# Issuing the TensorE and VectorE work of a full-attention loop in written order, score matmuls and PV matmuls each in one group per key tile

## The chip, the cores and the metric

The kernel runs on one core of a Trainium2 chip. The metric is the device time of one execution in microseconds (us), and a quoted time is the median of several executions. The mean granted TensorE clock, a fraction of full speed, is listed with each execution. Runs of one batch share a chip and the runs of the kernel before. TensorE is "PE" in the profile, VectorE is "DVE", ScalarE is "ACT", GpSimd is "POOL".

## The reference, cut to what matters

The program is four layers with residuals: a local dilated attention (A), a full attention with one shared key and value head (B), and the same two again. Only B is touched by the change. It has 2048 tokens, 32 query heads of 16 dimensions and one key/value head:

```python
def _B_ref(x, wq, wk, wv, wo):
    ...
    q = (x @ wq).reshape(B, S, H, Dh).transpose(0, 2, 1, 3)     # S = 2048, H = 32, Dh = 16
    k = x @ wk                                                  # one key head for all
    v = x @ wv
    scores = jnp.einsum("bhqd,bkd->bhqk", q, k) * (Dh ** -0.5)
    p = _softmax(scores, axis=-1)
    o = jnp.einsum("bhqk,bkd->bhqd", p, v)
    return o.transpose(0, 2, 1, 3).reshape(B, S, H * Dh) @ wo

x = x + _A_ref(_layernorm(x), A_wqkv, A_wo)
x = x + _B_ref(_layernorm(x), B_wq, B_wk, B_wv, B_wo)
x = x + _A_ref(_layernorm(x), A_wqkv, A_wo)
x = x + _B_ref(_layernorm(x), B_wq, B_wk, B_wv, B_wo)
```

## The kernel before

Each B layer is a loop of 512 steps: 32 blocks (512 queries of four heads each) times 16 key tiles of 128 keys. Per step the engines do this:

- TensorE computes four score tiles, each in its own quarter of the array's rows. Three go into a PSUM tile `st`, one into `dv`.
- ScalarE takes the exponential of the three in one instruction: `pt = exp(st)`.
- VectorE takes the fourth head's exponential by integer arithmetic. A "fix" (`tt` from `dv`, 512 columns) is done every step. A "pass" (`it` from `tt`, 2048 columns, covering four steps' fixes) is also done every step, four passes with different offsets for each group of four key tiles.
- TensorE multiplies by the values (PV): three matmuls of `pt` and four of `it`, each in its own quarter of the array's columns, all accumulating into `o_ps`.

So a step has 4 score and 7 PV matmuls, one exponential, one fix and one pass. There are two `st` buffers, one `dv` buffer and one `o_ps` buffer.

At the end of each block `finish_block` copies `o_ps` out on VectorE and sends the denominators on by DMA. After each second block it takes their reciprocals on VectorE and sends them out by DMA again, for a multiplication on GpSimd. The end of some blocks is followed by four output-projection matmuls ("y") and the addition of their result on VectorE.

The instructions are written in a sensible order, but in the kernel before they only carry data dependencies: the scheduler of the kernel language decides at build time in what order each engine gets them.

```python
def order_after(tc, inst, pred):
    if inst is not None and pred is not None:
        same = inst.ins.engine == pred.ins.engine
        tc.add_manual_dep(inst.ins, pred.ins.name, _ORDER if same else _AFTER, reason="issue order")
```

```python
    def emit_scores(s):
        b, kt, gd = where(s)
        qc, t, a = blocks[b]
        st = st_tiles[s] = stp.tile([128, 3, 512], F32, name="st")
        dv = dv_tiles[s] = dvp.tile([128, 512], F32, name="dv")
        outs = [(g, st[:, n, :]) for n, g in enumerate(g for g in range(4) if g != gd)] + [(gd, dv[:])]
        for g, out in outs:
            nc.tensor.matmul(out, lhsT=KAB[32 * g:32 * g + 32, a, kt * 128:(kt + 1) * 128],
                             rhs=QT[32 * g:32 * g + 32, t, qc * 512:(qc + 1) * 512],
                             start=True, stop=True, tile_position=(32 * g, 0))

    def emit_exp(s):
        pt = pt_tiles[s] = ptp.tile([128, 3, 512], BF16, name="pt")
        nc.scalar.activation(out=pt[:], in_=st_tiles.pop(s)[:], func=AF.Exp, scale=scale)

    def emit_fix(s):
        m, r = divmod(s, 4)
        if r == 0:
            t_tiles[m] = ttp.tile([128, 4, 512], I16, name="tt")
        nc.vector.tensor_scalar(out=t_tiles[m][:, r, :], in0=dv_tiles.pop(s)[:], scalar1=T_SCALE, scalar2=T_BIAS,
                                op0=ALU.mult, op1=ALU.add)

    def emit_pass(m, j):
        it = i_tiles[(m, j)] = itp.tile([128, 4, 512], BF16, name="it")
        nc.vector.tensor_scalar(out=it[:].bitcast(I16), in0=t_tiles[m][:], scalar1=0.25,
                                scalar2=127.0 * 128.0 + J_OFF[j], op0=ALU.mult, op1=ALU.add)
        if j == NJ - 1:
            del t_tiles[m]

    def pv(b, g, kt, j, rhs, stop):
        if b not in o_ps:
            o_ps[b] = opp.tile([128, 512], F32, name="o_ps")
        nc.tensor.matmul(o_ps[b][32 * g:32 * g + 32, :], lhsT=VE[:, kt, j, :], rhs=rhs,
                         start=(b, g) not in started, stop=stop, tile_position=(0, 32 * g))
        started.add((b, g))

    def emit_pv_act(s):
        b, kt, gd = where(s)
        pt = pt_tiles.pop(s)
        for n, g in enumerate(g for g in range(4) if g != gd):
            pv(b, g, kt, 0, pt[:, n, :], False)

    def emit_pv_dve(m, j):
        b, kt0, _ = where(4 * m)
        it = i_tiles.pop((m, j))
        for r in range(4):
            pv(b, r, kt0 + r, j, it[:, r, :], kt0 + 4 == NT and j == NJ - 1)

    # ... finish_block (the copy, the DMAs, the reciprocal) and emit_y cut ...
```

```python
    # ... pump() cut: it takes up to `budget` entries of the queue that are ready ...
    emit_scores(0)
    emit_fix(0)
    emit_scores(1)
    for s in range(nsteps + 8):
        if s < nsteps:
            emit_exp(s)
        if s + 1 < nsteps:
            emit_fix(s + 1)
        if s + 2 < nsteps:
            emit_scores(s + 2)
        m, j = divmod(s - 3, 4)
        if 0 <= s - pv_lag < nsteps:
            queue.append(("act", s, s - pv_lag))
        if 0 <= m < nsteps // 4:
            queue.append(("dve", s, (m, j)))
            if j == NJ - 1 and m % 4 == 3:
                queue.append(("end", s + 1, m // 4))
        if queue and queue[0][0] == "end":
            pump(s, 1)
        if 0 <= m < nsteps // 4:
            emit_pass(m, j)
        pump(s, pv_budget)
    while queue:
        pump(10 ** 9, 100)
    for qi in range(4):
        emit_y(NQC - 1, qi, (opp, dvp)[qi % 2], ("o_ps", "dv")[qi % 2])
```

`order_after` exists already. Between two instructions of one engine it fixes their order and adds no semaphore.

Of the kernel before, what the change touches and what calls it, by code (L numbers as in the profile page):

```python
# [8 lines left out]
I16 = mybir.dt.int16  # L9
# [467 lines left out]
def attn_B_fast(ctx, tc, QT, KAB, VE, wo_sb, x_sb, S, tag, out_dram=None, on_qc_done=None, st_bufs=2,  # L477
                pv_lag=3, y_gap=2, pv_budget=4):
    nc = tc.nc
# [20 lines left out]
    st_tiles, dv_tiles, pt_tiles, t_tiles, i_tiles = {}, {}, {}, {}, {}  # L500
    o_ps, started = {}, set()
    x_pair, onc = {}, {}

    def emit_scores(s):
        b, kt, gd = where(s)
        qc, t, a = blocks[b]
        st = st_tiles[s] = stp.tile([128, 3, 512], F32, name="st")
        dv = dv_tiles[s] = dvp.tile([128, 512], F32, name="dv")
        outs = [(g, st[:, n, :]) for n, g in enumerate(g for g in range(4) if g != gd)] + [(gd, dv[:])]
        for g, out in outs:  # L510
            nc.tensor.matmul(out, lhsT=KAB[32 * g:32 * g + 32, a, kt * 128:(kt + 1) * 128],  # L511
                             rhs=QT[32 * g:32 * g + 32, t, qc * 512:(qc + 1) * 512],
                             start=True, stop=True, tile_position=(32 * g, 0))

    def emit_exp(s):
        pt = pt_tiles[s] = ptp.tile([128, 3, 512], BF16, name="pt")
# [2 lines left out]
    def emit_fix(s):  # L519
        m, r = divmod(s, 4)  # L520
        if r == 0:
            t_tiles[m] = ttp.tile([128, 4, 512], I16, name="tt")
        nc.vector.tensor_scalar(out=t_tiles[m][:, r, :], in0=dv_tiles.pop(s)[:], scalar1=T_SCALE, scalar2=T_BIAS,  # L523
                                op0=ALU.mult, op1=ALU.add)

    def emit_pass(m, j):
        it = i_tiles[(m, j)] = itp.tile([128, 4, 512], BF16, name="it")
        nc.vector.tensor_scalar(out=it[:].bitcast(I16), in0=t_tiles[m][:], scalar1=0.25,  # L528
                                scalar2=127.0 * 128.0 + J_OFF[j], op0=ALU.mult, op1=ALU.add)
        if j == NJ - 1:  # L530
            del t_tiles[m]

    def pv(b, g, kt, j, rhs, stop):
        if b not in o_ps:
            o_ps[b] = opp.tile([128, 512], F32, name="o_ps")
        nc.tensor.matmul(o_ps[b][32 * g:32 * g + 32, :], lhsT=VE[:, kt, j, :], rhs=rhs,  # L536
                         start=(b, g) not in started, stop=stop, tile_position=(0, 32 * g))
        started.add((b, g))

    def emit_pv_act(s):  # L540
# [11 lines left out]
    def finish_block(b):  # L552
        qc, t, a = blocks[b]
        ops = o_ps.pop(b)
        if a == 0:
            X = nrm.tile([128, 512], F32, name="X")
            S2 = nrm.tile([128, 2, 16], F32, name="S2")
            x_pair[b // 2] = (X, S2)
            nc.vector.tensor_copy(out=X[:], in_=ops[:])  # L559
            src = X  # L560
        else:
            X, S2 = x_pair.pop(b // 2)
            src = nrm.tile([128, 512], F32, name="X1")
            nc.vector.tensor_copy(out=src[:], in_=ops[:])
        for g in range(4):
            nc.sync.dma_start(out=S2[32 * g:32 * g + 32, a, :], in_=src[32 * g + 16:32 * g + 17, :])  # L566
        if a == 0:
            return
        for g in range(4):
            nc.sync.dma_start(out=X[32 * g + 16:32 * g + 32, :], in_=src[32 * g:32 * g + 16, :])  # L570
        nc.vector.reciprocal(out=S2[:], in_=S2[:])
        rd = drm.tile([4, 2, 512], F32, name="rd")
        for g in range(4):
            nc.sync.dma_start(out=rd[g].rearrange("a (c e) -> c a e", e=16), in_=S2[32 * g:32 * g + 32, :, :])
        lb = nrm.tile([128, 512], F32, name="lb")
        for g in range(4):
            for aa in range(2):
                nc.sync.dma_start(out=lb[32 * g + 16 * aa:32 * g + 16 * aa + 16, :],
                                  in_=rd[g, aa:aa + 1, :].to_broadcast([16, 512]))
        if t == 0:  # L580
            onc[qc] = nrm.tile([128, 4, 512], BF16, name="onc")
        nc.gpsimd.tensor_tensor(out=onc[qc][:, t, :], in0=X[:], in1=lb[:], op=ALU.mult)  # L582
# [3 lines left out]
    def emit_y(qc, qi, pool, name):  # L586
        y = pool.tile([128, D], F32, name=name)
        for t in range(4):
            nc.tensor.matmul(y[:], lhsT=onc[qc][:, t, qi * 128:(qi + 1) * 128], rhs=wo_sb[:, t, :],  # L589
                             start=(t == 0), stop=(t == 3))  # L590
        qt = 4 * qc + qi
        if out_dram is not None:
            if qi == 0:
                xo[qc] = nrm.tile([128, 4, D], BF16, name="xo")
            nc.vector.tensor_tensor(out=xo[qc][:, qi, :], in0=x_sb[:, qt, :], in1=y[:], op=ALU.add)  # L595
        else:
            nc.vector.tensor_tensor(out=x_sb[:, qt, :], in0=x_sb[:, qt, :], in1=y[:], op=ALU.add)
        if qi == 3:
            del onc[qc]
            if out_dram is not None:  # L600
# [2 lines left out]
            if on_qc_done is not None:  # L603
                on_qc_done(qc)

    queue = []
    held = [0]

    def pump(now, budget):
        n = 0  # L610
# [21 lines left out]
    emit_fix(0)  # L632
    emit_scores(1)
    for s in range(nsteps + 8):
        if s < nsteps:
            emit_exp(s)
        if s + 1 < nsteps:
# [11 lines left out]
            pump(s, 1)  # L649
        if 0 <= m < nsteps // 4:  # L650
            emit_pass(m, j)
        pump(s, pv_budget)
    while queue:
        pump(10 ** 9, 100)
    for qi in range(4):
        emit_y(NQC - 1, qi, (opp, dvp)[qi % 2], ("o_ps", "dv")[qi % 2])


@with_exitstack
# [181 lines left out]
```

## Time and profile before

| | kernel before |
|---|---|
| time, four runs | median 1969.22 us (1967.03 to 1971.10) |
| first B loop, from first to last exponential | 734.8 us in the profiled execution, 1.435 us a step |
| second B loop | 736.1 us |
| between the loops (output projection, layer A, set-up of B) | 232.1 us |
| after the second loop | 27.8 us |

The profiled execution took 1960.04 us.

From the page of the kernel before: the busy time of each engine, and the chain of work that ended last by engine.

```profile
PE 1737.2 (89%) x14596; PEld 520.2 (27%) x14596; DVE 1672.4 (85%) x2657; ACT 1569.1 (80%) x1261; POOL 76.0 (4%) x104
...
DVE 44%; PE 41%; issue 6%; ACT 4%; SPq 2%; DMA 2%; POOL 1%; DVEq 0%; POOLq 0%; ACTq 0%
```

From the view of windows, the part of the first loop in which the mean clock rounds to 1.00 (one dip to 0.50, of 3.4 us at 655 us, lies in it). The columns are the window, its length, then the busy time (and number of instructions) of PE, PEld, DVE, ACT and POOL, then the granted clock, the DMA share and GB/s.

```profile
250.00:960.00 710.00, 664.51 (x5506) 155.22 (x5505) 665.32 (x1076) 684.45 (x498) 19.61 (x15) 1.00 0.05 10
```

TensorE is busy 664.51 of 710 us (94%), VectorE 94%, ScalarE 96%. None is full, and all three are close. The chain of waits says who hands over to whom. It is from 400 to 900 us, by line of the kernel: L511 is the score matmul, L517 the exponential, L523 the fix, L528 the pass, L536 the PV matmul.

```profile
by line: DVE tt L523 25.1%; DVE it L528 23.3%; PE o_ps L536 18.6%; PE dv L511 11.5%; PE st L511 8.3%; ACT pt L517 3.9%; issue 3.2%; SPq L566 1.6%; DVE X L559 0.6%; DVE st_next L50 0.6%; DMA S_7801<-X_8106 0.6%; DVE x_sb L597 0.4%; DMA S_907
```

The exponential, on ScalarE, is 3.9% of this chain. The chain goes to and fro between VectorE (48%) and TensorE (38%). The waits of the same stretch are listed as us in total, number of times, and the longest:

```profile
DVE tt L523 <- PE dv L511: 25.2, 53, 0.8
ACT pt L517 <- PE st L511: 18.4, 30, 1.0
PE dv L511 <- DVE tt L523: 17.4, 38, 0.9
```

Here VectorE waits for TensorE's `dv` and TensorE waits for VectorE's fix, in many short waits. The timeline shows what the scheduler's order looks like. The columns are start, length, engine, line, operation and tiles, and the count; lines of weight loads are left out.

```profile
1239.85 0.38 PE L511 MATMUL dv<-QT,KAB 32*128 32x512 bf16 x1
...
1240.16 0.40 PE L536 MATMUL o_ps<-it,VE 128*32 128x512 bf16 x4
1240.27 0.69 DVE L523 TENSOR_SCALAR tt<-dv 128x512 int16<-128x512 f32 x1 [0.17 <-PE dv L511]
...
1240.50 0.39 PE L511 MATMUL st<-QT,KAB 32*128 32x512 bf16 x3
...
1240.82 0.39 PE L536 MATMUL o_ps<-pt,VE 128*32 128x512 bf16 x1
1240.88 1.28 DVE L528 TENSOR_SCALAR it<-tt 128x2048 int16<-128x2048 int16 x2
...
1241.14 0.39 PE L511 MATMUL dv<-QT,KAB 32*128 32x512 bf16 x1
...
1241.46 0.39 PE L536 MATMUL o_ps<-pt,VE 128*32 128x512 bf16 x2
1241.46 0.60 PE L536 MATMUL o_ps<-it,VE 128*32 128x512 bf16 x4
...
1242.00 0.39 PE L511 MATMUL st<-QT,KAB 32*128 32x512 bf16 x3
1242.08 0.68 DVE L523 TENSOR_SCALAR tt<-dv 128x512 int16<-128x512 f32 x1
```

A single `dv` matmul stands alone at 1239.85. Four PV matmuls follow, then three `st`, one PV, one more `dv` alone, six PV, and three `st`. Each of these groups takes about 0.32 us until the next one starts (0.54 for the six), although up to four members of a group run side by side in the array. TensorE never stands still here: from this `dv` to the one two steps later, at 1242.86, it takes 3.01 us, 1.5 a step. On VectorE two passes follow each other (1240.88, x2) instead of a fix and a pass in turn, so the fix of the `dv` made at 1241.14 comes only at 1242.08, when the passes are done.

Last, ScalarE's own pace. The prediction takes it from a stretch of the timeline without a listed wait:

```profile
494.08 20.31 ACT L517 ACTIVATE pt<-st 128x1536 bf16<-128x1536 f32 x15 [0.49 <-PE st L511]
```

Fifteen exponentials took 20.31 us, and the last of them counts with its full recorded 1.45, so they start (20.31 - 1.45) / 14 = 1.347 us apart on average. This mean is not the floor. Of the 14 distances eleven are 1.330 to 1.335, two are 1.35, and one is 1.485 (from 506.08 to 507.56). That last one waited for its `st` matmuls, which ran from 507.06 to 507.45, but no wait is listed, because the record of the exponential before it is 1.54 us long and covers the gap. In the changed kernel, the first exponentials of these two lines are 16 steps apart:

```profile
247.94 2.87 ACT L522 ACTIVATE pt<-st 128x1536 bf16<-128x1536 f32 x2
269.22 3.08 ACT L522 ACTIVATE pt<-st 128x1536 bf16<-128x1536 f32 x2
```

That is 21.28 / 16 = 1.330 us from start to start. In both kernels this is by far the most frequent distance (within 5 ns, 393 of 1023 before and 828 after), and none is below 1.329. So 1.330 us is the floor of a step as long as ScalarE does this work.

### The profile page before, as it was taken

How to read it: one execution, taken by the hardware profiler on the slowest of the kernel's cores; microseconds unless marked ns; L12 is line 12 of the kernel's file. 1: busy time of each engine (PE TensorE's matmuls, PEld its weight loads, DVE VectorE, ACT ScalarE, POOL GpSimd, SP SyncE). 2: the span in 40 equal slices, each digit the busy share in tenths (PEclk: the TensorE clock that was granted, in tenths of full speed). 3: DMA queues.
4: the chain of work that ended last, by engine and by line, in shares of the span. 5: the costliest groups of instructions: out<-in, count | busy, mean ns of one | idle time of the engine just before them, and what ended most of it. 6: DMA issues, size and time to landing. Idle time of an engine off the chain costs nothing.

```text
span 1958.3 us, 35782 instructions
## 1 busy us (share of the span) xinstructions
PE 1737.2 (89%) x14596; PEld 520.2 (27%) x14596; DVE 1672.4 (85%) x2657; ACT 1569.1 (80%) x1261; POOL 76.0 (4%) x104
## 2 busy tenths in 40 slices
PE   5888799999999999989678888999999999999995
PEld 4443222222222222222163342222222222222221
DVE  4797589999999999999638966999999999999995
ACT  5232599999999999999652236999999999999994
POOL 2001000000000000000010010000000000000000
PEclk9999799999999999999889997999999999999998
DMA  3020000000000000000000000000000000000000
GB/s 98 2 45 1 1 7 13 10 10 10 10 10 10 10 10 10 10 9 12 17 3 2 2 2 1 10 10 10 10 10 21 10 10 10 22 12 15 20 10 21
DMA packets 48401, 25.22 MB, mean 13 GB/s; under 512 B 36320, under 2 KB 41440, under 8 KB 48096
## 3 DMA queue, kind: packets, MB, share of 16 engines
q1 hardware_dynamic: 48224, 22.80, 5.0%
q8 instruction: 118, 1.93, 0.4%
q14 instruction: 59, 0.48, 0.1%
HBM read 15.24 MB, written 2.62 MB: 9 GB/s over the span
## 4 chain that ended last, share of the span: by engine, by line
DVE 44%; PE 41%; issue 6%; ACT 4%; SPq 2%; DMA 2%; POOL 1%; DVEq 0%; POOLq 0%; ACTq 0%
DVE tt L523 18%; DVE it L528 16%; PE o_ps L536 15%; PE dv L511 9%; PE st L511 7%; PE ps L194 3%; ACT pt L517 2%; DVE prod L219 2%; PE y L275 2%; SPq L566 1%; PE ps L364 1%; DVE pv L263 1%; DVE ln_stats L89 1%; PE acc L266 1%; DVE X L559 1%
## 5 line engine op out<-in xcount | busy, mean ns | idle before, releaser
L517 ACT ACTIVATE pt<-st 128x1536 bf16<-128x1536 f32 x1024 | 1413.8, 1461 | 69.8 <-PE st L511 42.6
L523 DVE TENSOR_SCALAR tt<-dv 128x512 int16<-128x512 f32 x1024 | 700.8, 684 | 107.3 <-PE dv L511 96.2
L528 DVE TENSOR_SCALAR it<-tt 128x2048 int16<-128x2048 int16 x1024 | 699.6, 700 | 7.4
L536 PE MATMUL o_ps<-it,VE 128*32 128x512 bf16 x4096 | 648.0, 387 | 1.7 <-DVE it L528 1.5
L536 PE MATMUL o_ps<-pt,VE 128*32 128x512 bf16 x3072 | 513.9, 393 | 1.8 <-DVE xo L595 0.7
L511 PE MATMUL st<-QT,KAB 32*128 32x512 bf16 x3072 | 434.8, 390 | 32.3 <-ACT pt L517 26.2
L511 PE MATMUL dv<-QT,KAB 32*128 32x512 bf16 x1024 | 390.0, 381 | 59.1 <-DVE tt L523 47.4
L536 PEld LDWEIGHTS <-VE 128*32 128x32 bf16 x7168 | 166.9, 94 | 553.5 <-issue 544.7
L511 PEld LDWEIGHTS <-KAB 32*128 32x128 bf16 x4096 | 151.6, 91 | 584.8 <-issue 583.0
L219 DVE TENSOR_TENSOR prod<-Qch,Kch 128x4096 bf16<-128x4096 bf16 x32 | 72.4, 2278 | 56.1 <-ACT Kch L198 54.8
L99 ACT ACTIVATE xn<-x_sb,ln_nmr,ln_rstd 128x512 bf16<-128x512 f32 x44 | 33.7, 807 | 100.4 <-DVE ln_nmr L93 90.5
L582 POOL TENSOR_TENSOR onc<-X,lb 128x512 bf16<-128x512 f32 x32 | 42.0, 1312 | 1467.2 <-DMA lb<-rd 920.9
L194 PE MATMUL ps<-xnT,w_sb 128*32 128x512 bf16 x1536 | 88.8, 385 | 1.9 <-ACT Vch L198 1.9
L266 PE MATMUL acc<-pv,ident 128*128 128x512 bf16 x256 | 68.1, 399 | 15.8 <-DVE pv L263 10.3
L194 PEld LDWEIGHTS <-w_sb 128*32 128x32 bf16 x1536 | 77.6, 140 | 12.5 <-issue 7.3
L222 PE MATMUL lg<-prod,ident 128*128 128x512 bf16 x256 | 60.6, 379 | 18.8 <-DVE prod L219 18.8
L263 DVE TENSOR_TENSOR pv<-attn,Vch 128x2048 bf16<-128x2048 bf16 x64 | 73.2, 1217 | 0.9 <-PE acc L266 0.8
L268 ACT CAST Och<-acc 128x2048 bf16<-128x2048 f32 x8 | 14.9, 1866 | 71.6 <-PE acc L266 71.6
L224 ACT ACTIVATE L<-lg 128x512 f32<-128x512 f32 x16 | 9.6, 597 | 70.8 <-PE lg L222 70.8
L109 PE MATMUL pT<-ident,xn 128*128 128x128 bf16 x256 | 27.5, 255 | 38.9 <-ACT xn L99 26.9
L589 PE MATMUL o_ps<-woB_sb,onc 128*128 128x512 bf16 x112 | 31.3, 400 | 28.2 <-POOL onc L582 25.7
L266 PEld LDWEIGHTS <-ident 128*128 128x128 bf16 x256 | 25.4, 101 | 58.5 <-issue 23.8
(157 smaller groups left out, 600.1 us busy)
## 6 DMA issues: line engine op xcount, KB each, us to landing
lb<-rd SPq DMA_DIRECT2D x256, 32.0 KB, 1.8
xi<-in_A_x_dram SPq DMA_DIRECT2D x4, 512.0 KB, 5.7
wo_r_73<-in_A_wo_dram SPq DMA_DIRECT2D x4, 512.0 KB, 8.1
out_dram<-xo SPq DMA_DIRECT2D x4, 512.0 KB, 3.0
w_sb<-in_A_wqkv_dram SPq DMA_DIRECT2D x4, 384.0 KB, 8.3
wq_sb<-in_B_wq_dram SPq DMA_DIRECT2D x4, 128.0 KB, 2.2
woB_sb<-in_B_wo_dram SPq DMA_DIRECT2D x4, 128.0 KB, 2.6
X<-X_3114 SPq DMA_DIRECT2D x4, 32.0 KB, 2.9
```

Source lines behind the costliest of these rows:

```text
L194: nc.tensor.matmul(ps[32 * c:32 * c + 32, :], lhsT=wqkvP[:, kt, j, d, :], rhs=xnT[:, kt, c * 512:(c + 1) * 512], start=(kt == 0), stop=(kt ...
L219: nc.vector.tensor_tensor(out=prod[:], in0=Q[:, dsl, :], in1=K[:, dsl, PAD - DIL * w:PAD - DIL * w + 512], op=ALU.mult)
L222: nc.tensor.matmul(lg[:], lhsT=ident[:PCH, :PCH], rhs=prod[:, d, :], start=(hf == 0 and d == 0), stop=(hf == 1 and d == DP - 1))
L263: nc.vector.tensor_tensor(out=pv[:], in0=attn[:, w, :].unsqueeze(1).to_broadcast([PCH, DG, 512]), in1=V[:, ds_, PAD - DIL * w:PAD - DIL * ...
L266: nc.tensor.matmul(acc[:, i, :], lhsT=ident[:PCH, :PCH], rhs=pv[:, i, :], start=(w == 0), stop=(w == W - 1))
L275: nc.tensor.matmul(ys[c][:], lhsT=O[32 * c:32 * c + 32, d, i * 128:(i + 1) * 128], rhs=wo_r4[32 * c:32 * c + 32, d, :], start=(d == 0), st ...
L511: nc.tensor.matmul(out, lhsT=KAB[32 * g:32 * g + 32, a, kt * 128:(kt + 1) * 128], rhs=QT[32 * g:32 * g + 32, t, qc * 512:(qc + 1) * 512], ...
L517: nc.scalar.activation(out=pt[:], in_=st_tiles.pop(s)[:], func=AF.Exp, scale=scale)
L523: nc.vector.tensor_scalar(out=t_tiles[m][:, r, :], in0=dv_tiles.pop(s)[:], scalar1=T_SCALE, scalar2=T_BIAS, op0=ALU.mult, op1=ALU.add)
L528: nc.vector.tensor_scalar(out=it[:].bitcast(I16), in0=t_tiles[m][:], scalar1=0.25, scalar2=127.0 * 128.0 + J_OFF[j], op0=ALU.mult, op1=ALU ...
L536: nc.tensor.matmul(o_ps[b][32 * g:32 * g + 32, :], lhsT=VE[:, kt, j, :], rhs=rhs, start=(b, g) not in started, stop=stop, tile_position=(0 ...
L582: nc.gpsimd.tensor_tensor(out=onc[qc][:, t, :], in0=X[:], in1=lb[:], op=ALU.mult)
```

## The change

The intent is that TensorE runs two groups per step, four scores then seven PV, and that VectorE alternates fix and pass. `chain` ties every TensorE instruction of the loop behind the one written before it, and the same for VectorE (only the statistics for the next layer, which VectorE also computes, are left free). Because a strict order makes a late VectorE instruction block everything behind it, two things are put off: the reciprocal waits until four steps after the DMAs that feed it, and the addition of y until one step after its matmuls.

```diff
+    tail = {}
+
+    def chain(key, inst):
+        order_after(tc, inst, tail.get(key))
+        tail[key] = inst
 
     def emit_scores(s):
 ...
-            nc.tensor.matmul(out, lhsT=KAB[...], rhs=QT[...], start=True, stop=True, ...)
+            chain("pe", nc.tensor.matmul(out, lhsT=KAB[...], rhs=QT[...], start=True, stop=True, ...))
 ... (the same for the PV and y matmuls with "pe"; for fix, pass, copies, reciprocal and y-add with "dve") ...
     def finish_block(b):
 ...
-        nc.vector.reciprocal(out=S2[:], in_=S2[:])
+        later.append((cur[0] + 4, lambda: normalize(b, X, S2)))
+
+    def normalize(b, X, S2):
+        qc, t, a = blocks[b]
+        chain("dve", nc.vector.reciprocal(out=S2[:], in_=S2[:]))
 ...
     def emit_y(qc, qi, pool, name):
 ...
+        later.append((cur[0] + 1, lambda: add_y(qc, qi, y)))
 ...
     for s in range(nsteps + 8):
+        cur[0] = s
 ...
         if 0 <= m < nsteps // 4:
             emit_pass(m, j)
+        later.sort(key=lambda e: e[0])
+        run_later(s)
         pump(s, pv_budget)
```

More of the change, by code (lines that the diff above doesn't have):

```diff
@@ L510, in emit_scores @@
         for g, out in outs:
-            nc.tensor.matmul(out, lhsT=KAB[32 * g:32 * g + 32, a, kt * 128:(kt + 1) * 128],
-                             rhs=QT[32 * g:32 * g + 32, t, qc * 512:(qc + 1) * 512],
-                             start=True, stop=True, tile_position=(32 * g, 0))
+            chain("pe", nc.tensor.matmul(out, lhsT=KAB[32 * g:32 * g + 32, a, kt * 128:(kt + 1) * 128],
+                                         rhs=QT[32 * g:32 * g + 32, t, qc * 512:(qc + 1) * 512],
+                                         start=True, stop=True, tile_position=(32 * g, 0)))
     def emit_exp(s):
@@ L522, in emit_fix @@
             t_tiles[m] = ttp.tile([128, 4, 512], I16, name="tt")
-        nc.vector.tensor_scalar(out=t_tiles[m][:, r, :], in0=dv_tiles.pop(s)[:], scalar1=T_SCALE, scalar2=T_BIAS,
-                                op0=ALU.mult, op1=ALU.add)
+        chain("dve", nc.vector.tensor_scalar(out=t_tiles[m][:, r, :], in0=dv_tiles.pop(s)[:], scalar1=T_SCALE,
+                                             scalar2=T_BIAS, op0=ALU.mult, op1=ALU.add))
     def emit_pass(m, j):
         it = i_tiles[(m, j)] = itp.tile([128, 4, 512], BF16, name="it")
-        nc.vector.tensor_scalar(out=it[:].bitcast(I16), in0=t_tiles[m][:], scalar1=0.25,
-                                scalar2=127.0 * 128.0 + J_OFF[j], op0=ALU.mult, op1=ALU.add)
+        chain("dve", nc.vector.tensor_scalar(out=it[:].bitcast(I16), in0=t_tiles[m][:], scalar1=0.25,
+                                             scalar2=127.0 * 128.0 + J_OFF[j], op0=ALU.mult, op1=ALU.add))
         if j == NJ - 1:
@@ L535, in pv @@
             o_ps[b] = opp.tile([128, 512], F32, name="o_ps")
-        nc.tensor.matmul(o_ps[b][32 * g:32 * g + 32, :], lhsT=VE[:, kt, j, :], rhs=rhs,
-                         start=(b, g) not in started, stop=stop, tile_position=(0, 32 * g))
+        chain("pe", nc.tensor.matmul(o_ps[b][32 * g:32 * g + 32, :], lhsT=VE[:, kt, j, :], rhs=rhs,
+                                     start=(b, g) not in started, stop=stop, tile_position=(0, 32 * g)))
         started.add((b, g))
@@ L558, in finish_block @@
             x_pair[b // 2] = (X, S2)
-            nc.vector.tensor_copy(out=X[:], in_=ops[:])
+            chain("dve", nc.vector.tensor_copy(out=X[:], in_=ops[:]))
             src = X
@@ L563, in finish_block @@
             src = nrm.tile([128, 512], F32, name="X1")
-            nc.vector.tensor_copy(out=src[:], in_=ops[:])
+            chain("dve", nc.vector.tensor_copy(out=src[:], in_=ops[:]))
         for g in range(4):
@@ L588, in emit_y, with add_y @@
         for t in range(4):
-            nc.tensor.matmul(y[:], lhsT=onc[qc][:, t, qi * 128:(qi + 1) * 128], rhs=wo_sb[:, t, :],
-                             start=(t == 0), stop=(t == 3))
+            chain("pe", nc.tensor.matmul(y[:], lhsT=onc[qc][:, t, qi * 128:(qi + 1) * 128], rhs=wo_sb[:, t, :],
+                                         start=(t == 0), stop=(t == 3)))
+        later.append((cur[0] + 1, lambda: add_y(qc, qi, y)))
+    def add_y(qc, qi, y):
         qt = 4 * qc + qi
@@ L594, in emit_y @@
                 xo[qc] = nrm.tile([128, 4, D], BF16, name="xo")
-            nc.vector.tensor_tensor(out=xo[qc][:, qi, :], in0=x_sb[:, qt, :], in1=y[:], op=ALU.add)
+            chain("dve", nc.vector.tensor_tensor(out=xo[qc][:, qi, :], in0=x_sb[:, qt, :], in1=y[:], op=ALU.add))
         else:
-            nc.vector.tensor_tensor(out=x_sb[:, qt, :], in0=x_sb[:, qt, :], in1=y[:], op=ALU.add)
+            chain("dve", nc.vector.tensor_tensor(out=x_sb[:, qt, :], in0=x_sb[:, qt, :], in1=y[:], op=ALU.add))
         if qi == 3:
@@ L604, in emit_y, with run_later @@
                 on_qc_done(qc)
-    queue = []
-    held = [0]
+    queue, later = [], []
+    held, cur = [0], [0]
+    def run_later(now):
+        while later and later[0][0] <= now:
+            later.pop(0)[1]()
     def pump(now, budget):
@@ L654, in attn_B_fast @@
         pump(10 ** 9, 100)
+    run_later(10 ** 9)
     for qi in range(4):
         emit_y(NQC - 1, qi, (opp, dvp)[qi % 2], ("o_ps", "dv")[qi % 2])
+        run_later(10 ** 9)
 @with_exitstack
```

## The prediction

> **What bounds it now.** The two full-attention loops run from the first to the last exponential, 227 to 962 us and 1194 to 1930 us of the span (times of the exp line): 736 us for 512 key-tile steps each, 1.437 us a step. No engine is saturated: in 25 us windows ScalarE is busy 88% to 100%, TensorE 88% to 98%, VectorE 88% to 98%. Runs of exps in the timeline that waited for nothing keep 1.345 us (15 in 20.31 us, the last taking 1.45): ScalarE's floor. VectorE needs 0.60 us per instruction back to back, so 1.20 us a step plus about 0.09 for evictions, y-adds and statistics. The chain of waits between 400 and 947 us is 49% VectorE, 38% TensorE, 4% ScalarE: the loop is held by the order of TensorE and VectorE, not by work.
>
> TensorE's waste is visible. Scores use a quarter of the rows, PV a quarter of the columns; up to four share a pass. In the chain a group of one to four takes 0.32 us, seven PVs take 0.54, so each change of kind costs about 0.10 beyond the 0.216 a pass. The scheduler's order isolates dv (0.32 alone) from its three st (0.32) and splits PV, about 1.5 us per step (1240 to 1249 us), above ScalarE's floor. The Trainium skill, "TensorEngine Tiling (Array Packing)", Key Properties, says a change of tiling mode drains TensorE; the 0.10 us agrees.
>
> **What the change does.** No work is added or removed; order edges within an engine add no semaphores. TensorE gets 3 st + dv, then 3 + 4 PV: 0.32 + 0.54 = 0.86 us a step. VectorE alternates fix and pass; the reciprocal moves four steps behind its eviction (5.4 us; its transfer took about 4.9 at the longest seen), the y-add one step behind its matmuls.
>
> **Critical path.** The one-buffer dv loop: fix 0.68 + matmul 0.37 + hand-offs about 0.07 = 1.12 us, under 1.20. So ScalarE should bind, at 1.345. A block end delays VectorE by 0.6 us, a block with y by about 2 us within five steps; slack recovers 0.145 us per step, and the two st buffers tolerate roughly 1.5 us of lag. I allow 1.365 us a step. At the loop start the clock is 0.5 for 15 to 25 us; there a packed step costs 0.54 + 0.97 = 1.51 us against about 2.1.
> Per loop: 512 x 1.365 = 699, plus about 3 us for the start, against 736: 34 us less, 68 in both. Layers A and the tail are unchanged. 1970 - 68 = 1902 us.
>
> **Predicted: 1902 us, range 1884 to 1930. Faster by over 2%: 0.88; within 2%: 0.09; slower: 0.03.**
>
> **What shows it.** Cadence 1.35 to 1.38; ScalarE over 97% busy in the loop; TensorE's busy share there falls from about 94% to below 80%; no dv alone in the timeline; the chain of waits moves mostly to ScalarE.
>
> **What would make it wrong.** Less dense TensorE could lose its clock: at 655 us, after VectorE starved it, it was 0.5 for 3.4 us ("TensorE: Matmul & The Clock Gate", Part 1, describes such windows). A cold step of 1.51 us exceeds the floor; but it was warm again after one window of just this packed order. Second, strict order may let a late VectorE block TensorE at dv and so the next st, most in blocks with y, where VectorE is full (16 x 1.20 + 2.1 = 21.3 of 21.5 us).

## The result, and the profile after

The changed kernel takes 1881.82 us (median of four, 1877.27 to 1884.99) against 1969.22. The ratio is 0.9555 (95% interval 0.9532 to 0.9578), so it is faster by 4.4%. Ratios here are the mean time of one kernel's fast runs over that of the other's fast runs of the same rounds, so they are not quite the ratio of the quoted medians.

The time lies 2 us below the predicted range of 1884 to 1930, and 20 us below its centre of 1902.

| | before | before, again | after | after, again |
|---|---|---|---|---|
| profiled execution, us | 1960.04 | 1975.36 | 1884.99 | 1883.50 |
| mean granted clock | 0.971 | 0.956 | 0.968 | 0.970 |
| first loop | 734.8 | 741.9 | 695.7 | 698.0 |
| second loop | 736.1 | 739.0 | 693.2 | 691.7 |
| between the loops | 232.1 | 237.4 | 239.2 | 237.1 |
| after the second loop | 27.8 | 28.0 | 27.9 | 26.1 |

The two columns "again" are experiments described below, each a single execution, so their state is unknown. The mean loop is 737.95 us before and 694.65 us after. That is 43.3 us per loop or 86.6 in both, and the medians differ by 87.4. So the whole gain lies in the loops.

The lines of the page of the changed kernel:

```profile
PE 1506.5 (80%) x14548; PEld 582.1 (31%) x14596; DVE 1660.3 (88%) x2657; ACT 1536.1 (82%) x1261; POOL 80.8 (4%) x104
...
DVE 36%; ACT 28%; PE 19%; issue 12%; SPq 2%; DMA 2%; POOL 1%; DVEq 0%; POOLq 0%; ACTq 0%
```

The window of the first loop with the mean clock at 1.00 (here the dip of 3.4 us is at 846 us), columns as above:

```profile
250.00:915.00 665.00, 556.80 (x5425) 180.54 (x5434) 648.95 (x1061) 660.30 (x491) 22.10 (x15) 1.00 0.05 11
```

TensorE's busy share fell from 94% to 84%. VectorE rose to 97.6%, and ScalarE to 99.3% at 491 exponentials in 665 us. The count includes those that the window cuts; from start to start the mean is 1.358 us, against 1.429 in the window of the kernel before, and against the floor of 1.330. The chain of waits from 400 to 900 us follows. The change moved the lines: L516 is now the score matmul, L522 the exponential, L528 the fix (not the pass, as before), L533 the pass and L541 the PV matmul.

```profile
by line: ACT pt L522 26.6%; DVE tt L528 23.9%; DVE it L533 23.2%; issue 9.2%; PE o_ps L541 4.8%; PE st L516 3.4%; PE dv L516 2.2%; DVE X L564 1.5%; DVE x_sb L609 1.2%; SPq L571 0.9%; SPq L575 0.7%; DMA X<-X_8738 0.4%; DMA X<-X_6229 0.4%; DV
```

ScalarE's part rose from 3.9% to 26.6%, and TensorE's three lines fell from 38% to 10%. VectorE keeps 47%, so the chain did not move to ScalarE alone. The waits:

```profile
PE st L516 <- ACT pt L522: 51.7, 145, 0.6
PE dv L516 <- DVE tt L528: 8.0, 15, 1.1
PE o_ps L541 <- DVE it L533: 5.0, 18, 0.4
...
ACT pt L522 <- PE dv L516: 4.4, 8, 1.6
...
DVE tt L528 <- PE dv L516: 0.8, 1, 0.8
```

TensorE now waits mainly for ScalarE (51.7 us for a free `st`), which is the sign of an engine with slack. VectorE waits for `dv` once, for 0.8 us, where it waited 25.2 us before. The timeline, weight loads left out:

```profile
700.84 0.68 DVE L533 TENSOR_SCALAR it<-tt 128x2048 int16<-128x2048 int16 x1
700.91 0.39 PE L516 MATMUL st<-QT,KAB 32*128 32x512 bf16 x3
700.98 0.37 PE L516 MATMUL dv<-QT,KAB 32*128 32x512 bf16 x1
...
701.28 0.40 PE L541 MATMUL o_ps<-pt,VE 128*32 128x512 bf16 x3
701.44 0.68 DVE L528 TENSOR_SCALAR tt<-dv 128x512 int16<-128x512 f32 x1
701.58 0.40 PE L541 MATMUL o_ps<-it,VE 128*32 128x512 bf16 x4
...
702.04 0.68 DVE L533 TENSOR_SCALAR it<-tt 128x2048 int16<-128x2048 int16 x1
702.25 0.39 PE L516 MATMUL st<-QT,KAB 32*128 32x512 bf16 x3 [0.28 <-ACT pt L522]
```

This is the intended picture: three `st` and the `dv` together, then three and four PV together. The fix and the pass take turns on VectorE, and TensorE stands still for 0.28 us until ScalarE frees an `st`. Counted over the whole program, as unbroken runs of score matmuls and of PV matmuls on TensorE, there were 2.75 groups per step before and there are 1.89 now.

### The profile page after: what moved, and what is told of

Read it like the earlier page. It is cut to its first block, busy times and chain, and to the rows that moved or that the text cites. A ratio compares the mean times of both kernels' runs of the same rounds, so it can differ in the third digit from the quotient of the medians.

```text
span 1883.3 us, 35972 instructions
## 1 busy us (share of the span) xinstructions
PE 1506.5 (80%) x14548; PEld 582.1 (31%) x14596; DVE 1660.3 (88%) x2657; ACT 1536.1 (82%) x1261; POOL 80.8 (4%) x104
## 4 chain that ended last, share of the span: by engine, by line
DVE 36%; ACT 28%; PE 19%; issue 12%; SPq 2%; DMA 2%; POOL 1%; DVEq 0%; POOLq 0%; ACTq 0%
ACT pt L522 27%; DVE tt L528 12%; DVE it L533 12%; PE o_ps L541 4%; PE st L516 3%; PE ps L194 3%; DVE prod L219 2%; PE dv L516 2%; PE y L275 2%; PE ps L364 2%; SPq L571 1%; DVE X L564 1%; DVE pv L263 1%; PE acc L266 1%; DVE ln_stats L89 1%
## 5 line engine op out<-in xcount | busy, mean ns | idle before, releaser
L522 ACT ACTIVATE pt<-st 128x1536 bf16<-128x1536 f32 x1024 | 1380.4, 1742 | 21.1 <-PE dv L516 19.4
L528 DVE TENSOR_SCALAR tt<-dv 128x512 int16<-128x512 f32 x1024 | 701.6, 685 | 46.3 <-PE dv L516 12.5
L533 DVE TENSOR_SCALAR it<-tt 128x2048 int16<-128x2048 int16 x1024 | 711.6, 696 | 0.0
L516 PE MATMUL st<-QT,KAB 32*128 32x512 bf16 x3072 | 406.5, 386 | 201.3 <-ACT pt L522 183.6
L541 PE MATMUL o_ps<-it,VE 128*32 128x512 bf16 x4096 | 440.3, 387 | 17.3 <-DVE it L533 15.9
L541 PE MATMUL o_ps<-pt,VE 128*32 128x512 bf16 x3072 | 411.0, 392 | 5.9 <-DVE X L564 2.3
L516 PE MATMUL dv<-QT,KAB 32*128 32x512 bf16 x1024 | 390.8, 382 | 19.7 <-DVE tt L528 15.4
L541 PEld LDWEIGHTS <-VE 128*32 128x32 bf16 x7168 | 212.1, 93 | 530.8 <-issue 496.1
L516 PEld LDWEIGHTS <-KAB 32*128 32x128 bf16 x4096 | 161.9, 91 | 469.8 <-issue 454.7
L591 POOL TENSOR_TENSOR onc<-X,lb 128x512 bf16<-128x512 f32 x32 | 46.9, 1464 | 1379.2 <-DMA lb<-rd 1009.4
L109 PE MATMUL pT<-ident,xn 128*128 128x128 bf16 x256 | 29.1, 270 | 38.3 <-ACT xn L99 26.6
```

The source lines that it names most:

```text
L516: chain("pe", nc.tensor.matmul(out, lhsT=KAB[32 * g:32 * g + 32, a, kt * 128:(kt + 1) * 128], rhs=QT[32 * g:32 * g + 32, t, qc * 512:(qc + ...
L528: chain("dve", nc.vector.tensor_scalar(out=t_tiles[m][:, r, :], in0=dv_tiles.pop(s)[:], scalar1=T_SCALE, scalar2=T_BIAS, op0=ALU.mult, op1 ...
L533: chain("dve", nc.vector.tensor_scalar(out=it[:].bitcast(I16), in0=t_tiles[m][:], scalar1=0.25, scalar2=127.0 * 128.0 + J_OFF[j], op0=ALU. ...
L541: chain("pe", nc.tensor.matmul(o_ps[b][32 * g:32 * g + 32, :], lhsT=VE[:, kt, j, :], rhs=rhs, start=(b, g) not in started, stop=stop, tile ...
L591: nc.gpsimd.tensor_tensor(out=onc[qc][:, t, :], in0=X[:], in1=lb[:], op=ALU.mult)
```

## The experiments

Two theories stood at the start. The first, P, is that packing TensorE's groups is the cause: fewer changes of kind, less time per step, and the loop falls to ScalarE's floor. The second, O, is that the fixed order as such is the cause: VectorE's turns become regular, `dv` is free in time, and TensorE's packing is only a side effect. All diffs are against the changed kernel.

| run | median us | ratio to before | groups per step |
|---|---|---|---|
| the change | 1881.82 | 0.9555 | 1.89 |
| e1: only TensorE's order | 1983.46 | 1.0068 | 1.89 |
| e2: only VectorE's order | 2105.13 | 1.0692 | 2.61 |
| e9: neither order, deferrals kept | 1964.03 | 0.9983 | 2.75 |
| e6: both orders, no deferrals | 2070.54 | 1.0525 | – |
| e3: both orders, scores split in two parts | 2180.82 to 2379.02 | none | 3.62 |
| e4: both orders, scores split in three parts | 3190.93 | 1.6148 | 5.36 |
| e8: as e3, packed in 6 of 16 steps | 2035.51 | 1.0354 | 2.89 |
| e5: a third less exponential work | 1855.93 | 0.9431 | – |
| e10: warm clock at the ends of the loops | 1876.87 | 0.9534 | – |

The medians of the kernel before in the three batches were 1968.61 (e1 to e4), 1965.62 (e5, e6, e8) and 1968.43 (e9, e10).

### e1: only TensorE in written order

```diff
     def chain(key, inst):
+        if key != "pe":
+            return
         order_after(tc, inst, tail.get(key))
```

> The changed kernel with the order edges on TensorE only; VectorE is ordered by the scheduler again, which bunches two passes or two fixes. Its matmul order is the changed kernel's (1.89 groups of one kind per step, against 2.75 before). Theory P (packing: the gain is TensorE time saved by fewer, fuller groups): keeps most of it, 1880 to 1900 us. Rival O (regular order: a late fix holds dv and with it TensorE, so VectorE's order matters as much): 1920 to 1950 us, with exps waiting for dv or st.

Measured: 1983.46 us (1976.52 to 1983.74), ratio 1.0068 [1.0045, 1.0091], with the clock at 0.969. TensorE has exactly the packing of the changed kernel, 1.89 groups per step, and nothing of the gain. Both theories missed in size, P by 83 us from its upper end. The waits from 400 to 900 us (here L518 is the score matmul and L530 the fix):

```profile
PE dv L518 <- DVE tt L530: 86.2, 123, 2.0
...
DVE tt L530 <- PE dv L518: 40.6, 90, 0.8
```

TensorE waits 86.2 us for VectorE's fix, 123 times, where the changed kernel waits 8.0 us. The timeline (L535 is the pass, L571 the copy of `o_ps`; some lines left out) shows how:

```profile
699.77 1.29 DVE L535 TENSOR_SCALAR it<-tt 128x2048 int16<-128x2048 int16 x2
...
700.98 0.68 DVE L530 TENSOR_SCALAR tt<-dv 128x512 int16<-128x512 f32 x1
701.58 0.68 DVE L571 COPY X<-o_ps 128x512 f32<-128x512 f32 x1
701.72 0.37 PE L518 MATMUL dv<-QT,KAB 32*128 32x512 bf16 x1 [0.69 <-DVE tt L530]
...
702.18 0.68 DVE L530 TENSOR_SCALAR tt<-dv 128x512 int16<-128x512 f32 x1
```

VectorE does two passes in a row, then a fix, then the copy of a block's end, then the next fix. TensorE's `dv` matmul of the next step has to wait 0.69 us for the fix that frees the single `dv` buffer. In the strict order all TensorE work behind it waits too.

Packing alone gained nothing here. A strict TensorE needs a VectorE that keeps the same turn.

### e2: only VectorE in written order

```diff
     def chain(key, inst):
+        if key != "dve":
+            return
         order_after(tc, inst, tail.get(key))
```

> The changed kernel with the order edges on VectorE only; TensorE is ordered by the scheduler (2.61 groups per step). Theory P: little gain, 1935 to 1970 us, TensorE busy above 92% in the loop. Rival O: at least half of the gain, below 1925 us.

Measured: 2105.13 us (2099.21 to 2108.82), ratio 1.0692 [1.0665, 1.0718], at a mean clock of 0.86. Both theories missed: it is slower than either allowed. Two windows of the first loop, columns as above:

```profile
400.00:450.00 50.00, 48.50 (x328) 10.73 (x327) 37.96 (x62) 39.97 (x29) 1.43 (x1) 0.69 0.03 8
500.00:550.00 50.00, 45.83 (x394) 13.53 (x388) 47.62 (x80) 46.75 (x35) 1.27 (x1) 1.00 0.05 12
```

At 500 us the clock is 1.00 and the window holds 35 exponentials (1.43 us a step, as before the change). At 400 us its mean is 0.69, TensorE is busy 97%, and the window holds 29. The mean clock of such windows lies between 0.69 and 0.81 from 250 to 450 us. In the clock record this is a change to and fro between 1.00 and 0.50, with cold stretches of 14 to 21 us. There a step takes 50 / 29 = 1.72 us with TensorE nearly full, which suggests that TensorE limits it. Why this kernel falls back to half clock so much more often than the kernel before, at nearly the same number of groups, is open.

e1 and e2 together show that neither order is worth anything alone, and that both are needed.

### e9: the deferrals alone

```diff
     def chain(key, inst):
-        order_after(tc, inst, tail.get(key))
-        tail[key] = inst
+        return
```

> The changed kernel with its two deferrals but no order edges at all: the scheduler orders both engines, and its matmul order has 2.75 groups per step as before. If the deferrals gain anything by themselves: 1940 to 1960 us. If the gain lies in the two orders together, which runs e1 and e2 suggest (each alone lost 0.7% and 7%): within 8 us of the kernel before.

Measured: 1964.03 us (1961.54 to 1970.71), ratio 0.9983 [0.996, 1.0007]: the same as before. Its window of the first loop is the same too; before had 664.51, 665.32 and 684.45 us of PE, DVE and ACT:

```profile
250.00:960.00 710.00, 667.60 (x5528) 156.05 (x5530) 665.02 (x1077) 684.46 (x498) 21.30 (x15) 1.00 0.05 10
```

Without order edges the written place of the reciprocal and the y-add has no lasting effect. By themselves the deferrals gain nothing.

### e6: both orders, no deferrals

```diff
-        later.append((cur[0] + 4, lambda: normalize(b, X, S2)))
+        normalize(b, X, S2)
 ...
-        later.append((cur[0] + 1, lambda: add_y(qc, qi, y)))
+        add_y(qc, qi, y)
```

> The changed kernel without its two deferrals: the reciprocal follows its eviction at once, the y-add follows its matmuls at once, in the fixed order. Theory: in a fixed order VectorE must sit out the transfer of the row sums, about 4.5 us, of which some 1 us is absorbed, 32 times, and the y matmuls 24 times; 1980 to 2030 us, with VectorE waiting for S2 and o_ps. Rival (the deferrals are tidiness): within 15 us of the changed kernel.

Measured: 2070.54 us (2062.43 to 2073.44), ratio 1.0525 [1.0481, 1.0569], at a mean clock of 0.906. VectorE's waits from 400 to 900 us (L580 is the reciprocal):

```profile
DVE S L580 <- DMA S<-X: 37.5, 10, 4.6
```

The reciprocal waits for its DMA ten times, for 3.75 us on average and 4.6 at the longest, and in written order nothing passes it. The changed kernel has no such wait in its list. The y-addition waits 5.6 us for its matmuls, so of the two deferrals, which e6 takes away together, that of the reciprocal seems to matter most. The direction was expected, the size was larger. One stall, in which VectorE stands still for 3.64 us until 422.86, in windows of 3 to 4 us:

```profile
419.00:422.00 3.00, 0.54 (x7) 0.19 (x4) 0.22 (x1) 2.38 (x2) 0.00 (x0) 1.00 0.03 2
422.00:426.00 4.00, 2.19 (x19) 0.53 (x18) 3.04 (x6) 0.92 (x1) 0.00 (x0) 0.60 0.18 35
426.00:430.00 4.00, 4.00 (x33) 0.62 (x29) 3.32 (x6) 3.79 (x4) 0.00 (x0) 0.55 0.16 51
430.00:434.00 4.00, 3.62 (x36) 0.93 (x33) 3.89 (x7) 4.00 (x4) 1.80 (x1) 1.00 0.06 16
```

VectorE is busy 0.22 us from 419 to 422 us and TensorE 0.54. From 422 to 430 us the mean clock is then 0.60 and 0.55 (in the clock record, 0.50 for 6.8 us), and only afterwards 1.00 again. So this stall cost its own time and 6.8 us of half clock on top. Over the span the mean clock is 0.906 where the changed kernel has 0.968. So the deferrals belong to the change: without them the strict order loses 5% instead of gaining 4.4%.

### e3 and e4: both orders, more groups per step

e3 writes the scores in two parts, so that a step is `dv`, three PV of `pt`, three `st`, four PV of `it`. e4 also puts one `st` between the PV of `pt`. The instructions are the same, only TensorE's order differs.

```diff
 ... (emit_scores split into parts; comments added here) ...
+        if s + 2 < nsteps:
+            emit_score_part(s + 2, (3,))            # dv alone
+            if queue and queue[0][0] == "act":
+                pump(s, 1)                          # three PV of pt
+            emit_score_part(s + 2, (0, 1, 2))       # three st
         if 0 <= m < nsteps // 4:                    # then four PV of it
```

```diff
 # e4, in addition to e3
         for n, g in enumerate(g for g in range(4) if g != gd):
+            if n == 1 and between:
+                between.pop()()                     # one st after the first PV of pt
             pv(b, g, kt, 0, pt[:, n, :], False)
 ... (the loop hands the st matmul to `between`) ...
```

> Both engines in a fixed order, VectorE as in the changed kernel, but TensorE alternates on purpose: dv | 3 PV of ScalarE | 3 st | 4 PV of VectorE, 3.62 groups per step over the program. Theory P: 4 x 0.32 = 1.28 us of TensorE per step, just under ScalarE's 1.345, so 1.36 to 1.42 us a step, total 1885 to 1945 us, TensorE busy about 95%. Rival O: same as the changed kernel within 10 us, since the order is as regular.

> As e3 with six groups a step: dv | 1 PV | 1 st | 2 PV | 2 st | 4 PV, 5.36 groups per step over the program. Same work, fixed order. Theory P: TensorE needs 6 x 0.32 = 1.92 us a step and becomes the bound, so about 0.56 us more per step for 1024 steps, total 2380 to 2480 us, chain of waits on TensorE. Rival O: within 20 us of the changed kernel.

Measured, e3: 2180.82 to 2379.02 us at clocks of 0.811 to 0.715. Only the fastest of its four runs counts as fast, so no ratio is formed; the profiled run is the slowest, of 2379.02 us, so its windows show how e3 runs, and not how often. Measured, e4: 3190.93 us (3153.91 to 3264.4), ratio 1.6148 [1.6055, 1.6241], at a clock of 0.69. All four expectations missed: none allowed for the clock. Two windows of e3, one of each loop:

```profile
300.00:350.00 50.00, 49.49 (x260) 9.84 (x257) 31.96 (x50) 33.20 (x24) 1.27 (x1) 0.50 0.04 9
1950.00:2000.00 50.00, 47.75 (x406) 14.39 (x403) 48.54 (x78) 49.07 (x37) 1.27 (x1) 1.00 0.07 15
```

In the second window the clock is 1.00 and 37 exponentials fit in 50 us, about 1.35 us a step: the pace of the changed kernel with twice its groups. In the first the clock is 0.50 throughout, TensorE is busy 99% by the records, and 24 exponentials fit, 2.1 us a step. That is close to what four groups cost at half clock, 4 x 0.54 = 2.16 us. It stayed so from the start of the first loop to about 550 us.

In e4 a step takes 1.85 us with a warm clock (27 exponentials from 750 to 800 us) and 3.1 cold (16 from 300 to 350), against 6 x 0.32 = 1.92 and 6 x 0.54 = 3.24. So the cost per group, 0.32 warm and 0.54 cold, holds in two orders that were made for the purpose. With a warm clock four regular groups just fit under ScalarE's floor and six do not.

This corrects the picture of the kernel before. Four groups in a regular order run at about 1.35 us when the clock is warm, and the kernel before has 2.75 groups and runs at 1.43. An estimate from the costs measured here (0.32 for the first pass after a change, 0.216 for each further pass) agrees: over the loops its groups add up to 1.12 us a step, those of e3 to 1.24, both under the floor of 1.330. So the number of groups was not what held a warm step at 1.43 on average, though it could in stretches like the one at 1240 us. That points to the irregular turns of the two engines. What packing does give is slack. At 0.54 + 0.97 = 1.51 us a packed step exceeds the floor by only 0.18 even at half clock, while four groups at 2.16 fall far behind. The cold start of the loops shows it: the first 16 steps take 0.7 us more than 16 times the floor in the changed kernel, and 4.6 to 6.4 us more in the kernel before.

### e8: four groups, but packed in six of sixteen steps

```diff
+            if s % 16 in range(8, 14):
+                emit_score_part(s + 2, (0, 1, 2, 3))    # packed, as in the changed kernel
+            else:
+                ...                                     # the order of e3
```

This asks whether a few packed steps in each block bring the clock back.

> As e3 (four groups a step) but with six of every 16 steps, the ones after a block end, in the packed order of the changed kernel. Theory B (the clock has two stable states: a warm loop stays warm even with four groups, a cold one only warms when the groups are full, so the packed stretch brings it back after each block end): 1890 to 1990 us, warm nearly throughout, mean clock above 0.93. Rival D (the clock follows the mean density of the order): still cold for about half of the loops, 2050 to 2200 us, mean clock near 0.85.

Measured: 2035.51 us (2025.62 to 2046.74), ratio 1.0354 [1.0295, 1.0414], clock 0.90. That is between the two expectations. Two neighbouring windows of 25 us:

```profile
400.00:425.00 25.00, 24.36 (x162) 5.20 (x158) 18.18 (x29) 19.93 (x15) 0.00 (x0) 0.65 0.01 1
425.00:450.00 25.00, 21.53 (x202) 7.22 (x201) 24.17 (x40) 24.49 (x19) 1.68 (x1) 1.00 0.09 18
```

The clock recovers within a block, from 0.65 to 1.00, as the theory B of the quoted text has it, and no cold stretch lasts longer than 24 us where e3's first lasted for 328. But it drops again more often than B assumed. Packed steps help the clock return, while the four-group steps lose it again.

### e5: a third less work for ScalarE

```diff
-        nc.scalar.activation(out=pt[:], in_=st_tiles.pop(s)[:], func=AF.Exp, scale=scale)
+        nc.scalar.activation(out=pt[:, 0:2, :], in_=st_tiles.pop(s)[:, 0:2, :], func=AF.Exp, scale=scale)
 ...
-            pv(b, g, kt, 0, pt[:, n, :], False)
+            pv(b, g, kt, 0, pt[:, min(n, 1), :], False)
```

The result is wrong (relative error 0.16). The run only asks what limits the changed kernel after ScalarE.

> The changed kernel with the exponential of two heads of three (1024 of 1536 columns; PV reads the second head's twice, so the result is wrong on purpose). ScalarE then needs about 0.92 us a step. Theory S (ScalarE alone bounds the changed loop at 1.356 us a step): VectorE's 1.29 us is next, so about 0.065 us less per step, 1805 to 1830 us, VectorE above 97% busy in the loop. Rival H (the handshake of TensorE and VectorE over the one dv buffer holds the loop near 1.35 and a full ScalarE is a coincidence): 1870 to 1890 us, ScalarE near 70% busy.

Measured: 1855.93 us (1850.66 to 1859.6), ratio 0.9431 [0.9397, 0.9466]. So only about 26 us are gained. The window of its first loop and its chain of waits from 400 to 900 us (L533 pass, L528 fix):

```profile
250.00:900.00 650.00, 607.97 (x5378) 154.22 (x5387) 636.82 (x1053) 494.92 (x486) 21.46 (x15) 0.99 0.05 11
```

```profile
by line: DVE it L533 40.8%; DVE tt L528 40.3%; SPq L571 3.6%; DMA X<-X 2.9%; issue 2.6%; PE o_ps L541 1.9%; DVE X L564 1.6%; SPq L575 1.6%; DVE X L569 1.5%; DVE x_sb L609 1.1%; DVE S L580 0.6%; PE st L516 0.4%; PE dv L516 0.4%; DVEq L528 0.
```

ScalarE falls to 76%, VectorE is at 98%, and 81% of the chain is fix and pass. The time lies between the two expectations. VectorE is next, as the theory S has it, but it needs more than assumed: the window holds 486 exponentials, 1.337 us a step, where 1.29 had been estimated. The start times show where the 0.05 comes from. One fix in four, the first into a new `tt` tile, starts 0.79 us after the pass before it and not 0.60 (628.01 to 628.80 us in e5); it also carries a wait for a semaphore of VectorE's own. That is 0.19 / 4 = 0.05 us a step, in gaps too short for the list of waits.

Taken apart by blocks of 16 steps, the start times also show which engine limits where. In the twelve blocks of a loop whose steps contain y matmuls, a step takes 1.38 us in the changed kernel (mean of its four profiled loops) and 1.37 in e5: less exponential work gains nothing there. In the other blocks (the first left out) it takes 1.34 (medians 1.331 to 1.334, close to ScalarE's floor), and 1.31 in e5. So ScalarE limits most blocks and VectorE those with y, and this explains why the chain of the changed kernel is shared between them.

### b0 and a0: both kernels once more

The kernel before and the changed kernel were each run once more with a profile, with no edit, because the first profile of the kernel before came from an unusually fast execution.

> The kernel before, profiled again, to see how far its loops vary: the first profile was of an execution of 1960 us, the timed ones are near 1969. If the first profile was a favourable one: 1966 to 1972 us, with one loop or both 4 to 8 us longer than 736 us, by cold stretches of the clock. If the loops are constant: 736 us each, the difference in layers A.

> The changed kernel, profiled again, for the spread of its loops and of the time between them (first profile: 695.7, 239.2 and 693.2 us). If the 7 us that the time between the loops grew belong to the change: 237 to 241 us again. If they are the clock's luck (before showed 232.1 and 237.4): anything from 231 to 240. Loops 692 to 698 us.

Measured: 1975.36 us, a little more than either expectation, and 1883.50 us; the table of the result has their parts. The kernel before had loops of 741.9 and 739.0 us this time, with cold stretches inside the loop (clock 0.80 and 0.73 in 25 us windows between 290 and 415 us) that its first profile did not have. The time between the loops, which looked as if the change had lengthened it by 7 us (232.1 to 239.2), is 237.4 and 237.1 us this time. Over all thirteen profiled runs it lies between 232.1 and 239.2. So a lengthening by the change is not shown.

### e10: keeping the clock up between the loops

```diff
+    y_part((0, 1, 2))          # three quarters of the last y matmuls before the last normalization
+    fill(TAIL_FILL)            # 50 matmuls into a scratch tile
     run_later(10 ** 9)
+    y_part((3,))
 ...
+    if out_dram is None:
+        fill(END_FILL)         # 40 more, after the first loop only
```

In the changed kernel the 16 y matmuls after the first loop run cold, from 939.5 to 945.2 us. This version starts most of them early and fills TensorE's wait.

> The changed kernel plus a different end of each loop: the y matmuls of the first three head groups run while the last transfer is on its way, and 50 unused matmuls behind them (40 more after the first loop) keep the clock up. If the cold clock and the serial y matmuls at the loop ends cost what the profile shows (16 cold y matmuls 5.7 us, a cold start of layer A some 5 us): 8 to 16 us less than the changed kernel, 1866 to 1874 us, the time between the loops from 239 to 226 to 232 us. If not: within 4 us of the changed kernel.

Measured: 1876.87 us (1871.35 to 1882.76, five runs), ratio 0.9534 [0.9512, 0.9556], with 233.7 us between the loops at a clock of 0.95, against 239.2 and 237.1 us at 0.88 and 0.90. That is between the two expectations. It is about 5 us less than the change in the medians. The intervals of the two ratios overlap, so it is not shown to beat the changed kernel.

## Why the prediction was right or wrong, point by point

The prediction had the direction, and ScalarE as the limit of most of the loop. It was wrong in size: 1902 us was predicted and 1881.8 measured, 20 us lower and 2 us below the range.

**The step that failed** is the cost "1.345 us", called "ScalarE's floor", on which "I allow 1.365 us a step" rests. The floor is 1.330. The 15 exponentials "that waited for nothing" contain one hidden wait and two slightly longer distances, and the mean took them in. At 512 steps the error is 512 x 0.015 = 7.7 us a loop. The prediction makes a loop 512 x 1.345 + 512 x 0.020 + 3 = 702 us, and the four measured loops of the changed kernel average 694.65, which is 7.3 us less. So the rest of the sum held: 10.2 + 3 = 13.2 us were allowed above the floor, and 694.65 - 512 x 1.330 = 13.7 us were needed. That was partly luck. The cold start took about 0.7 us and not 3, while the rest of the loop took some 13 us and not 10.2, about 10 of them in the twelve blocks with y.

**A smaller error lies in the base.** The gain was computed from loops of 736 us in one profiled execution of 1960 us, but subtracted from a timed median of 1970. The four measured loops of the kernel before average 737.95 us, another 2 x 1.95 = 3.9 us. The two errors, 2 x 7.3 = 14.7 and 3.9, are 18.6 of the 20.2 us. The remainder is 1.6 us, within the spread of single executions.

The other points:

- *"ScalarE should bind, at 1.345."* Half right: it binds at 1.330, in the blocks without y (medians 1.331 to 1.334 us a step). In those with y VectorE binds (1.38), as the prediction's last paragraph feared.
- *"TensorE's busy share there falls from about 94% to below 80%."* The direction was right, the size was not: it fell to 84%. The page "Perfetto Trace Analysis" of the Trainium skill, section "Identifying the Most-Contended Engine", says that TensorE's busy share does not measure how close it is to its limit, because pipelined matmuls look smaller in the trace. e3 has TensorE at 99% with 260 matmuls in 50 us and at 95.5% with 406 (at half and at full clock).
- *"Cadence 1.35 to 1.38."* Right: 695.7 / 512 = 1.359 and 693.2 / 512 = 1.354.
- *"No dv alone in the timeline."* Nearly right: the groups are intact, but a `dv` still starts late around y matmuls (at 602.63 us, for instance).
- *"The chain of waits moves mostly to ScalarE."* Half right: 26.6%, with 47% for VectorE. e5 shows why: VectorE's need of "1.20 us a step plus about 0.09" was mis-sized. It is 1.337 when VectorE limits, so the two engines are almost equally full, and "slack recovers 0.145 us per step" was too hopeful in the blocks with y.
- *"The reciprocal moves four steps behind its eviction."* Right, and it matters more than the prediction said: without it and the deferral of y, e6 lost 5.25% against the kernel before.
- *The danger named first, a lost clock.* It did not happen to the changed kernel (0.968 and 0.970 over the whole span), but it happened in e2, e3, e4, e6 and e8. The mechanism was named and its reach was not seen.
- *The emphasis on "TensorE's waste".* The prediction's account leads from the cost of a change of kind to the gain. The Trainium skill, "TensorEngine Tiling (Array Packing)", Key Properties, says that changing the tiling mode drains TensorE, and e4 agrees with a cost per group of 0.32 us warm, 0.10 beyond a pass. But e1 has all the packing and none of the gain, and e3 has twice the groups and, when warm, all of the pace. What is shown is that the gain needs TensorE's order, VectorE's order and the deferrals together (e1, e2, e6, e9). How the gain would divide between packing and regularity cannot be told from these runs, because every version with regular turns and unpacked groups lost its clock.

The kept traces say more of the clock than the runs were built for. The clock record of each has only the values 1.00 and 0.50, and changes at multiples of 3.4 us. For each such window inside the loops of all thirteen traces (those with y matmuls left out) we can count the matmuls that start in it. Of the cold windows, all 116 with 24 or more were followed by full clock; of those with 20 to 23, 45 of 137; of those with fewer, 5 of 1082. The recorded busy share does not tell them apart: 995 windows that were busy 95% or more stayed cold. At half clock a packed step puts 11 matmuls into 1.51 us, which is 25 per window, and four groups put them into 2.16 us, which is 17. This fits the changed kernel, e3 and e8. The fall goes with idle time: of the warm windows, all 50 that were busy less than 57.7% were followed by half clock, and none of the 3355 above 79.3%. These are counts made afterwards, and no run tested them by itself. It stays open why e2 and the kernel before, which lie between (about 20 per window by the same estimate), differ so much.

## What to carry to other kernels

When three engines are all over 90% busy and the chain of waits goes to and fro between two of them, look at the order in which they take turns, before looking for work to remove. Fix the order on all engines of the loop at once and put off whatever waits for a DMA, because a strict order on one engine alone makes it wait for the irregularity of the other (1983 us against 1882 here). Take the base of an estimate from the same kind of execution as the time it is subtracted from, and check a second profile before trusting the first to 1%. Read an engine's floor from the shortest and most frequent distance between starts, not from the mean of a stretch that looks free of waits: 0.015 us a step was 15 us here.

## What the Trainium skill lacked or had wrong

- "TensorE: Matmul & The Clock Gate", Part 1, "What's actually happening", gives full clock after one busy window of about 3.4 us. e3 held the clock at 0.50 for about 300 us with TensorE recorded as busy 97% to 99% (windows from 300 to 550 us; 260 matmuls in 50 us). So "busy" there cannot mean the recorded busy share; over all traces 995 cold windows recorded as busy 95% or more were not followed by full clock. The changed kernel, in packed order, came back from a dip after a single such time (clock 0.50 from 846.0 to 849.4 us, 1.00 after it), as the page has it.
- "TensorEngine Tiling (Array Packing)", Key Properties, says that a change of tiling mode drains TensorE and gives no size. Here a group of one to four concurrent tiles of 512 columns takes 0.32 us from group to group at full clock and 0.54 at half, against 0.216 and 0.43 for a further pass in the same group. So a change costs about 0.10 us.
- "Perfetto Trace Analysis", "Summary: the profiler window per engine type", says that the recorded window of ScalarE runs through the write acknowledgement. No page says that it can grow while the pace improves. The exponential's recorded mean rose from 1461 to 1742 ns (section 5 of the pages) while a warm step of the first loop fell from 1.429 to 1.358 us, and the shortest distance from start to start stayed at 1.330 us. Such records hid a wait (1.485 us between two starts under a record of 1.54).
- No page says what strict order on one engine does when the other keeps a scheduler's order: 1983 us with TensorE's order alone, 2105 with VectorE's alone, 1882 with both.
